# Three buffers instead of two for the keys, queries and values of a head pair

## The chip, the cores and the metric

The kernel runs on one core of a Trainium2 chip (trn2). Such a core has TensorE (PE in the profile, PEld for its weight loads), VectorE (DVE), ScalarE (ACT), GpSimd (POOL), SyncE (SP), which here only issues DMAs, and 16 DMA engines. The time is the device time of one execution in microseconds (us). The profile is a record of one such execution.

## What is computed

Three layers on 1536 tokens (2 batches of 768), in float32: attention with 8 heads of 64, in which a query sees itself and the `n_local` - 1 = 95 positions before it, and the first `n_global` = 8 keys; an MLP with a normalised input; and a layer of 8 experts, of which each token takes one.

```python
rel = pos[:, None] - pos[None, :]
is_global = pos[None, :] < int(n_global)
is_local = (rel >= 0) & (rel < int(n_local))
...
scores = scale * np.matmul(q, k.transpose(0, 1, 3, 2)) + bias   # bias: -slope of the head * distance
scores = np.where(is_global | is_local, scores, -1000000000.0)
a = np.exp(scores - np.max(scores, axis=-1, keepdims=True))
a = a / (np.sum(a, axis=-1, keepdims=True) + 1e-09)
x = np.matmul(a, v)                       # then heads side by side: 1536 x 512
...
xn = x / rms * rms_g
x = (silu(xn @ w_gate) * (xn @ w_val)) @ w_out          # 512 -> 1536 -> 512
...
out[mask] = gate_w[mask, None] * (np.maximum(x[mask] @ w1[e], 0.0) @ w2[e])   # expert e's tokens
```

## The kernel before

**Tiling.** The tokens are cut into 12 tiles of 128 rows and the tiles into six stages of two (`SIZES`). The attention works on a stage and a pair of heads at a time: 6 stages x 4 head pairs = 24 pairs, numbered 0 to 23 in the order `order`. A unit is one tile of a pair, so there are 48. A tile of queries needs at most two blocks of 128 keys: its own, and the one before it, of which the first 32 columns are replaced by the global keys.

**One pair.** `prep(gi)` makes pair gi ready. Its loads put transposed keys into `kn`, transposed queries into `qn`, and values into `vn`, in which two further columns are set to one by POOL (L432), so that the value matmuls also give the sums of the exponentials. Pairs 0 to 7 are "raw": scores come straight from `kn` and `qn` in float32 (L533, L537, L538). For pairs 8 to 23 each operand is split into a rounded part, copied by ACT (L486 keys, L498 queries), and a remainder (POOL L489 for the keys, DVE L499 for the queries), in `kt` and `qt`; the scores are then L550. POOL copies the windows with the global keys and values (L421).

**Buffers.** Pairs 0 to 3 are loaded at the very start into row tiles of the later output (`part`) that are still unused. From pair 4 on `kn`, `qn` and `vn` come from tags with two buffers each. `prep(0)` asks for the loads of pairs 4 and 5, and `prep(gi)` from gi = 4 on for those of pair gi + 2. A load can be issued when the last reader of the tile that had the buffer is through: for `kn` of a raw pair its score matmuls, of a later pair its copy and remainder; for `vn` the pair's value matmuls.

**One unit.** `scores` (TensorE, into the two banks "s"), a fused add and minimum on DVE (L557), the exponential on ACT (L561); two units later `turn`, four or two transposes on TensorE (L572) and a copy by ACT (`ptS`, L580); some three units later `values` (L601) into the one bank `xp`. Behind a pair's second unit DVE adds 1e-9 to the sums, takes reciprocals (L608, L609) and multiplies (L611, one instruction for each of the two tiles) into the row tiles `part`, which are the halves of `duo`. When four pairs of a stage are done, `tail` normalises the rows, transposes them (L400) and splits them (L403, L404) for the MLP.

**Order.** All DMAs of the attention and of the weights are issued from SP's one queue. Each engine takes its instructions in a fixed order. This order is laid down when the program is built: a planner (`schedule_with_timeline_sim=True`, L1375) goes through the program text in its order, simulates the engines, and puts an instruction into its engine's queue when its inputs and its buffer are free in that simulation. Between the units of the attention the text has steps of the first MLP pass (`moe_block`, L769 and L806) for stages whose rows are ready; steps that convert the MLP's weights (`convert64`, L334 to L354, raw data in the ring of tiles "raw", three buffers) are put in at fixed units. For the first 16 units TensorE also runs filler matmuls (`warm`).

**At the start**, before the branch that begins the body, DVE and POOL make the distance tables from two scalars that a DMA brings; `tri_f`, a triangle of ones, is made by POOL and cast to `tri` by DVE (L137, L138, L142), for the routing much later. The global keys are loaded in float32 into `kgn` in `prep(0)` and are split in `prep(2)` (L451, L452).

Of the kernel before, what the change touches and what calls it, by code (L numbers as in the profile page):

```python
# [8 lines left out]
F32 = mybir.dt.float32  # L9
# [5 lines left out]
ALU = mybir.AluOpType  # L15
# [4 lines left out]
P = 128  # L20
B, H, S, D = 2, 8, 768, 64
NT, DM, DFF = B * S, H * D, 1536
NE, DF2 = 8, 1024
KD = DM // P
NP = H // 2
# [4 lines left out]
STARTS = [sum(SIZES[:i]) for i in range(len(SIZES))]  # L30
NSTAGE = len(SIZES)
ST = ST_MAX = max(SIZES)
STAGE = ST * P
TB = S // P
VW = 2 * (D + 1)
NM = DFF // P
GW = 32
# [8 lines left out]
def kernel(  # L46
# [16 lines left out]
    nc = tc.nc  # L63
    slope = [2.0 ** (-(h + 1)) for h in range(H)]
    NFP, LATE = 4, 8
    NRAWG = 8
    XT = "ccccss"
    RING = "ccceewweec"
# [8 lines left out]
    NRAW = 3  # L77
# [24 lines left out]
    const = ctx.enter_context(tc.tile_pool(name="const", bufs=1))  # L102
# [16 lines left out]
        out=nval, in0=nneg, scalar=4294967296.0, in1=nf[:, :, 0], op0=ALU.mult, op1=ALU.add  # L119
# [7 lines left out]
        out=flagf[:, 2:3], in0=nval[0:1, 1:2], scalar=float(LMAX), in1=flagf[:, 1:2], op0=ALU.is_le, op1=ALU.mult  # L127
# [5 lines left out]

    gB = const.tile([P, DM], F32, name="gB")
    rg = const.tile([P, KD, NE], F32, name="rg")
    tri_f = const.tile([P, P], F32, name="tri_f")
    nc.gpsimd.memset(tri_f, 1.0)  # L137
    nc.gpsimd.affine_select(  # L138
        out=tri_f, in_=tri_f, pattern=[[1, P]], compare_op=ALU.is_gt, fill=0.0, base=0, channel_multiplier=-1
    )  # L140
    tri = const.tile([P, P], BF16, name="tri")
    nc.vector.tensor_copy(tri, tri_f)  # L142
    ones = const.tile([P, P], BF16, name="ones")
    nc.vector.memset(ones, 1.0)
    ie_i = const.tile([P, NE], I32, name="ie_i")
# [21 lines left out]
    rp = ctx.enter_context(tc.tile_pool(name="rp", bufs=1))  # L167

    def behind(i, first):

        tc.add_manual_dep(
            i.ins, first.ins.name,
            mybir.DependencyInfo(mybir.DependencyClass.NoSync, mybir.DependencyReason.DATA), reason="order",
        )


    def warm(n, after=None):
        for _ in range(n):
            w = psum.tile([P, 512], F32, tag="mm", bufs=NMM, name="warm")
            i = nc.tensor.matmul(  # L180
                out=w.rearrange("p (a n) -> p a n", a=4), lhsT=wz, rhs=wz.unsqueeze(1).to_broadcast([P, 4, P]),
                start=True, stop=True,
            )
            if after is not None:
                behind(i, after)
# [13 lines left out]
    def is_raw(st, hp):  # L199
        return st * NP + hp < NRAWG  # L200

    def load_pair(st, hp, kn, qn, vn):
        b, t0, nt = STARTS[st] // TB, STARTS[st] % TB, SIZES[st]
        i0 = 0 if t0 else 1
        nk = nt + 1 - i0
        k0 = (t0 - 1 + i0) * P
        hd = slice(P * hp, P * (hp + 1))
        if is_raw(st, hp):
            nc.sync.dma_start(out=kn[:, 0:nk * P], in_=kT[b][hd, k0:k0 + nk * P])
            nc.sync.dma_start(out=qn[:, 0:nt * P], in_=qT[b][hd, t0 * P:(t0 + nt) * P])  # L210
            nc.sync.dma_start(
                out=rows_of(vn)[:, i0:i0 + nk, 1:P + 1],
                in_=v[b, k0:k0 + nk * P, hd].rearrange("(t p) c -> p t c", p=P),
            )
            return kn, qn, vn
        for x, src in ((kn[:, 0:2 * nk * P], kT[b][hd, k0:k0 + nk * P]), (qn[:, 0:2 * nt * P], qT[b][hd, t0 * P:(t0 + nt) * P])):
            for r in range(2):
                nc.sync.dma_start(
                    out=x[D * r:D * (r + 1), :].rearrange("d (j s) -> d j s", j=2),
                    in_=src.rearrange("(j d) s -> d j s", j=2),  # L220
                )
        nc.sync.dma_start(
            out=rows_of(vn)[:, i0:i0 + nk, 1:P + 1],
            in_=v[b, k0:k0 + nk * P, hd].rearrange("(t p) c -> p t c", p=P),
        )
        return kn, qn, vn
# [7 lines left out]
    duo = [rp.tile([P, 2, DM], F32, name=f"duo{i}") for i in range(TT // 2)]  # L234
    part = [duo[i // 2][:, i % 2] for i in range(TT)]
# [46 lines left out]
    for x in (tab0, tabL, tabG):  # L282
        half = const.tile([P, x.shape[1]], F32, name="half" + str(len(tabs)))
        nc.scalar.activation(out=half, in_=x, func=ACTF.Copy, scale=0.5)
        tabs.append((x, half))

    warm(WARM0)
    fast = nc.values_load(flag, min_val=0, max_val=1)

    def body(is_fast):  # L290
# [9 lines left out]
        def ps(tag, bufs, name):  # L300
            return psum.tile([P, 512], F32, tag=tag, bufs=bufs, name=name)
# [108 lines left out]
        def fast_attention(pool):  # L410
            kg = pool.tile([P, NP, 2, GW], F32R, name="kg")

            kgr = pool.tile([P, NP, GW], F32, name="kgr") if NRAWG > NP else None
            kgn = pool.tile([P, NP, 2, GW], F32, name="kgn")
            vg = pool.tile([P, P], F32, name="vg")
            groups = []
            loaded = list(first_pairs)
# [5 lines left out]
            def prep(gi):  # L423
                st, hp = order[gi]
                t0, nt = STARTS[st] % TB, SIZES[st]
                i0 = 0 if t0 else 1
                n = nt * P
# [6 lines left out]
                for gn in nxt:  # L434
                    if gn >= len(order):
                        break
                    nat = [
                        pool.tile([P, 2 * STAGE if x == "q" else 2 * DM if x == "k" else (ST_MAX + 1) * VW], F32, tag=f"{x}n", bufs=2, name=f"{x}n") for x in "kqv"
                    ]
                    loaded.append(load_pair(*order[gn], *nat))  # L440
                nk = nt + 1 - i0
                if gi == 0:
                    kg0 = kT[0].rearrange("(h d) s -> d h s", d=D)[:, :, 0:GW]
                    for r in range(2):
                        nc.sync.dma_start(
                            out=kgn[D * r:D * (r + 1)].rearrange("d a j s -> d (a j) s"), in_=kg0
# [3 lines left out]
                if gi == 2:  # L450
                    nc.scalar.activation(out=kg, in_=kgn, func=ACTF.Copy)  # L451
                    nc.gpsimd.tensor_tensor(  # L452
                        out=kg[D:P], in0=kgn[D:P], in1=kg[D:P].bitcast(F32), op=ALU.subtract
# [4 lines left out]
                f = 1 if t0 >= 2 else 3 - t0  # L458
# [34 lines left out]
                if hi_dve[1]:  # L493
                    nc.vector.tensor_scalar(
                        out=qhi, in0=srq, scalar1=0.125 / slope[2 * hp], scalar2=None, op0=ALU.mult
                    )
                else:
                    nc.scalar.activation(out=qhi, in_=srq, func=ACTF.Copy, scale=0.125 / slope[2 * hp])  # L498
                lo_eng[kq[1]].scalar_tensor_tensor(  # L499
                    out=qt[:, :, 1, 0:n], in0=srq, scalar=0.125 / slope[2 * hp], in1=qhi.bitcast(F32),  # L500
# [84 lines left out]
            def values(g, t, ptf, nb):  # L585
                st, t0, hp, qt, kt, vn, vx, mx = groups[g]
                nt = SIZES[st]
                if t == 0:
                    xps[g] = ps("x", 1, "xp")
                xp = xps[g]  # L590
                for j in range(2):
                    c = slice(j * (D + 1), (j + 1) * (D + 1))
                    o = xp[:, t * VW + j * (D + 1):t * VW + (j + 1) * (D + 1)]
                    for a in range(nb):
                        if nb == 1 or a == 1:
                            rhs = vn[:, t + 1, c]
                        elif t0 + t == 1:
                            rhs = vn[:, t, c]
                        else:
                            rhs = vx[:, t, c]  # L600
                        nc.tensor.matmul(  # L601
                            out=o, lhsT=ptf[:, (j * nb + a) * P:(j * nb + a + 1) * P], rhs=rhs,
                            start=(a == 0), stop=(a == nb - 1),
                        )
                if t == nt - 1:
                    rc = pool.tile([P, ST, 2], F32, tag="rc", bufs=2, name="rc")
                    xs3 = xp[:, 0:nt * VW].rearrange("p (t c) -> p t c", c=VW)
                    nc.vector.tensor_scalar(out=rc[:, 0:nt], in0=xs3[:, :, 0:VW:VW - 1], scalar1=1e-9, scalar2=None, op0=ALU.add)  # L608
                    nc.vector.reciprocal(rc[:, 0:nt], rc[:, 0:nt])  # L609
                    for tt in range(nt):  # L610
                        nc.vector.tensor_tensor(  # L611
                            out=part[STARTS[st] + tt][:, hp * P:(hp + 1) * P].rearrange("p (j d) -> p j d", j=2),
                            in0=xp[:, tt * VW + 1:tt * VW + 1 + P].rearrange("p (j d) -> p j d", j=2),
                            in1=rc[:, tt].unsqueeze(2).to_broadcast([P, 2, D]), op=ALU.mult,
                        )
                    groups[g] = None

            warm(WARM1)
            prep(0)
            yield "work"  # L620
            tails = []
            q1, q2 = [], []
            n = hold = 0
            while n < len(units) or q1 or q2:
# [18 lines left out]
                if last is not None:  # L643
                    g, t = last
                    if t == SIZES[g // NP] - 1 and g % NP == NP - 1:
                        st = g // NP
# [518 lines left out]
        while True:  # L1165
# [12 lines left out]
            while True:  # L1178
                if moe is None and ready:
                    st = ready.pop(0)  # L1180
# [45 lines left out]
        for a in range(KD):  # L1226
            raw = rp.tile([P, P, NE], F32, tag="raw", bufs=NRAW, name="rawg")
            nc.sync.dma_start(out=raw, in_=r_gate[a * P:(a + 1) * P, :].partition_broadcast(P))
            for h in range(2):
                nc.scalar.activation(  # L1230
                    out=rgb[h][:, :, a * P:(a + 1) * P],
                    in_=raw[:, :, 4 * h:4 * h + 4].rearrange("p d e -> p e d"), func=ACTF.Copy,
# [33 lines left out]
        st, ms = NSTAGE - 1, range(M1, NM)  # L1266
        prep_next(0, first, len(first))
        banks["mm"] = MMC.split()
        with tc.manual_schedule(engines={mybir.EngineType.PE}):
# [10 lines left out]
            x = expert_tile(w1t[0], w2t[0], tka, wta, xsa, lambda: None, True)  # L1280
# [21 lines left out]
        for e in range(NE):  # L1302
# [17 lines left out]
            if e == 0:  # L1320
                x = expert_tile(w1t.pop(0), w2t.pop(0), tks[:, 0:1], wts[:, 0:1], xs.pop(0), between)
# [58 lines left out]
```

## Time and profile before

| | |
|---|---|
| Median of 3 runs | 655.97 us (655.12 to 656.81) |
| Profiled execution | 655.69 us |
| Its span in the trace | 654.0 us, so 1.69 us lie around it |
| TensorE busy | 628.9 us, 96% of the span |
| DVE, ACT, POOL busy | 446.2, 320.3, 208.7 us |
| Mean granted clock of TensorE | 0.988 of full speed |

The times of the trace are counted from the start of the span. A row of the timeline gives the start, the length (to the end of the last, where several alike are merged), the engine, the line, the operation with what it writes and reads, and in brackets how long the engine stood idle before it and what ended that. Ends of matmuls are modelled, so a busy TensorE is not one at its peak.

### The profile page before, as it was taken

To read this page: it belongs to the slowest core of one execution; us is meant where nothing else is said; L and a number is where in the kernel's file an instruction comes from. 1 tells how busy PE (TensorE), PEld (TensorE's weight loads), DVE (VectorE), ACT (ScalarE), POOL (GpSimd) and SP (SyncE) were. 2 spreads that over 40 slices of the span, in tenths; PEclk is the share of its full clock that TensorE was granted. 3 is DMA by queue.
4 is the path that set the end of the run, shared out by engine and by line. 5 is a ranking of instruction groups with operands and counts; after the bars stand their busy time and mean duration, and the time that the engine had idled before them with its cause. 6 is when DMAs were issued, how large, how long until landed. Compare 5 with 4: busy or idle time off the path is not lost. (4 is left out here: it accounts for less than half of the span.)

```text
span 654.0 us, 11691 instructions
## 1 busy us (share of the span) xinstructions
PE 628.9 (96%) x4280; PEld 562.3 (86%) x4281; DVE 446.2 (68%) x1098; ACT 320.3 (49%) x624; POOL 208.7 (32%) x275
## 2 busy tenths in 40 slices
PE   9998998899999999999999999999999999999992
PEld 4667887899999999999999999997888899899891
DVE  5765888976599988676359998944667464664410
ACT  3666798777555533334622221333656564654420
POOL 4415758663122212111222532461610221011010
PEclk9999899899999999999999999999999999999997
DMA  7536466551044532131311010442978667454000
GB/s 228 158 90 201 127 174 181 157 149 39 1 130 130 161 98 72 59 98 65 129 65 65 2 65 34 122 138 82 301 261 261 206 217 253 168 189 140 17 13 30
DMA packets 56567, 82.98 MB, mean 127 GB/s; under 512 B 7983, under 2 KB 38703, under 8 KB 56496
## 3 DMA queue, kind: packets, MB, share of 16 engines
q1 hardware_dynamic: 53552, 74.75, 36.9%
q0 software_dynamic: 2944, 7.35, 3.4%
q8 instruction: 37, 0.61, 0.4%
q14 instruction: 34, 0.28, 0.1%
HBM read 75.75 MB, written 7.39 MB: 127 GB/s over the span
## 5 line engine op out<-in xcount | busy, mean ns | idle before, releaser
L769 PE MATMUL pg<-xn,gv 128*128 128x256 f32 x1728 | 228.2, 285 | 1.2 <-DVE th L778 1.2
L769 PEld LDWEIGHTS pg<-xn,gv 128*128 128x128 f32 x1728 | 220.2, 192 | 8.2 <-DVE th L778 1.5
L787 POOL TENSOR_TENSOR hid<-hf,hid 128x256 fp32r<-128x256 f32 x72 | 61.4, 855 | 174.6 <-ACT hid L786 174.5
L806 PE MATMUL po<-ow,hid 128*128 128x512 f32 x432 | 113.9, 394 | 0.0
L1017 PE MATMUL py<-ew,eh 128*128 128x512 f32 x384 | 91.2, 395 | 0.9 <-DVE eh L1084 0.5
L1017 PEld LDWEIGHTS py<-ew,eh 128*128 128x128 f32 x384 | 71.3, 188 | 17.7 <-DVE eh L1084 0.9
L806 PEld LDWEIGHTS po<-ow,hid 128*128 128x128 f32 x432 | 75.5, 189 | 11.7 <-POOL hid L787 0.3
L1039 PE MATMUL ph<-xs,ew 128*128 128x256 f32 x672 | 83.1, 283 | 0.0
L1039 PEld LDWEIGHTS ph<-xs,ew 128*128 128x128 f32 x672 | 81.6, 191 | 0.7
L786 ACT ACTIVATE hid<-hf 128x256 fp32r<-128x256 f32 x72 | 29.9, 417 | 83.7 <-DVE hf L782 81.9
L1024 POOL DMA_INDIRECT out_dram<-yo,tk x16 | 16.5, 1034 | 139.1 <-ACT yo L1023 107.7
L838 DVE CUSTOM_DVE_ANT_0 jk<-duo,rgb 128x512 bf16<-128x512 f32 x64 | 54.3, 849 | 0.5
L561 ACT ACTIVATE pr<-pr,mx 128x256 f32<-128x256 f32 (+1 forms) x96 | 45.1, 484 | 14.0 <-DVE mx L557 13.2
L957 DVE TENSOR_TENSOR ew<-rawe,ew 128x1024 fp32r<-128x1024 f32 (+1 forms) x36 | 40.8, 1134 | 12.9 <-ACT ew L953 12.9
L1048 DVE SCALAR_TENSOR_TENSOR eh<-ph,eh 128x256 fp32r<-128x256 f32 x56 | 23.1, 423 | 37.5 <-ACT eh L1047 35.5
L777 ACT ACTIVATE th<-pg 128x256 f32<-128x256 f32 x72 | 27.2, 379 | 39.8 <-PE pg L769 37.3
L957 DVE TENSOR_TENSOR ew<-duo,ew 128x1024 fp32r<-128x1024 f32 x28 | 34.1, 1224 | 17.9 <-ACT ew L953 16.8
L953 ACT ACTIVATE ew<-rawe 128x1024 fp32r<-128x1024 f32 x36 | 38.0, 1059 | 10.2 <-PE pg L769 4.6
L778 DVE SCALAR_TENSOR_TENSOR th<-th,pg 128x256 f32<-128x256 f32 x72 | 29.7, 415 | 16.4 <-ACT th L777 15.4
L1047 ACT ACTIVATE eh<-ph 128x256 fp32r<-128x256 f32 x56 | 21.2, 384 | 39.2 <-PE ph L1039 38.1
L953 ACT ACTIVATE ew<-duo 128x1024 fp32r<-128x1024 f32 x28 | 29.4, 1059 | 19.4 <-PE py L1017 19.4
L815 DVE TENSOR_TENSOR duo<-duo,po 128x512 f32<-128x512 f32 x36 | 23.4, 684 | 18.7 <-PE po L806 18.6
(178 smaller groups left out, 935.8 us busy)
## 6 DMA issues: line engine op xcount, KB each, us to landing
rawe<-in_moe_w_dram SPq DMA_DIRECT2D x36, 512.0 KB, 5.0
duo<-in_moe_w_dram SPq DMA_DIRECT2D x28, 512.0 KB, 5.4
raw<-in_moe_w_gate_dram SPq DMA_DIRECT2D x12, 512.0 KB, 3.8
raw<-in_moe_w_val_dram SPq DMA_DIRECT2D x12, 512.0 KB, 5.6
raw<-in_moe_w_out_dram SPq DMA_DIRECT2D x12, 512.0 KB, 3.4
kn<-in_k_dram SPq DMA_DIRECT2D x28, 192.0 KB, 3.3
qn<-in_q_dram SPq DMA_DIRECT2D x36, 128.0 KB, 2.9
vn<-in_v_dram SPq DMA_DIRECT2D x16, 192.0 KB, 2.6
```

The source lines that it names most:

```text
L561: pin["act"] = nc.scalar.activation(out=pr[:, j, 0:n], in_=pr[:, j, 0:n], func=ACTF.Exp, bias=mx[:, t, j:j + 1], scale=-1.0,)
L769: nc.tensor.matmul(out=pg[:, 0:n_], lhsT=gv[:, i, a, kk, :], rhs=x[st][:, kk, :], start=(n == 0), stop=(n == 3 * KD - 1),)
L777: pin["th"] = nc.scalar.activation(out=th, in_=pss[0][:, 0:n_], func=ACTF.Tanh, scale=0.5)
L778: nc.vector.scalar_tensor_tensor(out=th, in0=th, scalar=1.0, in1=pss[0][:, 0:n_], op0=ALU.add, op1=ALU.mult)
L786: nc.scalar.activation(out=hh[:, 0], in_=hf, func=ACTF.Copy)
L787: nc.gpsimd.tensor_tensor(out=hh[:, 1], in0=hf, in1=hh[:, 0].bitcast(F32), op=ALU.subtract)
L806: nc.tensor.matmul(out=po, lhsT=hid[mi][:, a, t * P:(t + 1) * P], rhs=ow[:, c, :], start=(mi == 0 and n == 0), stop=(mi == len(ms) - 1 and ...
L838: nc.vector.tensor_tensor_reduce(out=jk, in0=part[i0 + t], in1=rgb[e // 4][:, e % 4, :], scale=1.0, scalar=0.0, op0=ALU.mult, op1=ALU.add, ...
L953: cp = nc.scalar.activation(out=t[:, 0], in_=raw, func=ACTF.Copy)
L957: nc.vector.tensor_tensor(out=t[:, 1, 0:nd], in0=raw[:, 0:nd], in1=t[:, 0, 0:nd].bitcast(F32), op=ALU.subtract)
L1017: last_mm["py"] = nc.tensor.matmul(out=py, lhsT=hid(m, a, j), rhs=w2t[m // 2][:, c, (m % 2) * DM:(m % 2 + 1) * DM], start=(n == 0), stop=( ...
L1039: nc.tensor.matmul(out=ph[:, 0:CAP], lhsT=w1t[kk][:, a, m * P:(m + 1) * P], rhs=x[:, kk, :], start=(n == 0), stop=(n == 3 * KD - 1),)
```

## The change

- The tags of `kn`, `qn` and `vn` have three buffers each (`NKN`, `NQN`, `NVN`). `kn` is cut from 1024 to 768 columns, which is what three key blocks of two heads need. What `prep` asks for, and when, stays: pair gi + 2.
- `kgn` is no tile of its own; it lies in the first 256 columns of row tile 2.
- `tri_f` is made after the tables, in a tile of the ring "raw", which is used there for the fourth time (after `ri`, `rel` and `keep`).
- A pair's two products L611 become one instruction over both tiles, 128 x 256 elements.

```diff
+    NKN, NQN, NVN = 3, 3, 3
...
-    tri_f = const.tile([P, P], F32, name="tri_f")
-    nc.gpsimd.memset(tri_f, 1.0)
-    nc.gpsimd.affine_select(
-        out=tri_f, in_=tri_f, pattern=[[1, P]], compare_op=ALU.is_gt, fill=0.0, base=0, channel_multiplier=-1
-    )
...
-    nc.vector.tensor_copy(tri, tri_f)
...
+    tri_f = rp.tile([P, P], F32, tag="raw", bufs=NRAW, name="tri_f")
+    nc.gpsimd.memset(tri_f, 1.0)
+    nc.gpsimd.affine_select(
+        out=tri_f, in_=tri_f, pattern=[[1, P]], compare_op=ALU.is_gt, fill=0.0, base=0, channel_multiplier=-1
+    )
+    nc.vector.tensor_copy(tri, tri_f)
...
-            kgn = pool.tile([P, NP, 2, GW], F32, name="kgn")
+            kgn = part[2][:, 0:2 * NP * GW].rearrange("p (a j s) -> p a j s", a=NP, j=2)
...
                     nat = [
-                        pool.tile([P, 2 * STAGE if x == "q" else 2 * DM if x == "k" else (ST_MAX + 1) * VW], F32, tag=f"{x}n", bufs=2, name=f"{x}n") for x in "kqv"
+                        pool.tile([P, w], F32, tag=f"{x}n", bufs=nb, name=f"{x}n")
+                        for x, w, nb in (
+                            ("k", 2 * (ST_MAX + 1) * P, NKN), ("q", 2 * STAGE, NQN), ("v", (ST_MAX + 1) * VW, NVN)
+                        )
                     ]
...
-                    for tt in range(nt):
-                        nc.vector.tensor_tensor(
-                            out=part[STARTS[st] + tt][:, hp * P:(hp + 1) * P].rearrange("p (j d) -> p j d", j=2),
-                            in0=xp[:, tt * VW + 1:tt * VW + 1 + P].rearrange("p (j d) -> p j d", j=2),
-                            in1=rc[:, tt].unsqueeze(2).to_broadcast([P, 2, D]), op=ALU.mult,
-                        )
+                    nc.vector.tensor_tensor(
+                        out=duo[st][:, :, hp * P:(hp + 1) * P].rearrange("p t (j d) -> p t j d", j=2),
+                        in0=xs3[:, :, 1:P + 1].rearrange("p t (j d) -> p t j d", j=2),
+                        in1=rc[:, 0:nt].unsqueeze(3).to_broadcast([P, nt, 2, D]), op=ALU.mult,
+                    )
```

## Rows read from the trace of the kernel before

**Rows 1.** Stretches of the span: busy us (instructions) of PE, PEld, DVE, ACT, POOL; clock, DMA.

```profile
60.00:110.00 50.00, 45.03 (x342) 41.69 (x342) 40.93 (x130) 40.40 (x91) 33.24 (x48) 0.97 0.61 166
...
110.00:165.00 55.00, 51.40 (x405) 49.54 (x404) 41.27 (x126) 40.89 (x86) 32.87 (x50) 0.97 0.42 116
...
165.00:620.00 455.00, 453.39 (x3086) 415.79 (x3085) 321.10 (x682) 201.12 (x367) 114.11 (x115) 1.00 0.39 127
```

**Rows 2.** The same view in slices of 5 us.

```profile
60.00:65.00 5.00, 2.81 (x25) 2.68 (x25) 1.17 (x7) 2.72 (x6) 1.78 (x1) 1.00 0.80 221
...
65.00:70.00 5.00, 5.00 (x32) 5.00 (x32) 4.05 (x7) 4.65 (x11) 4.04 (x8) 0.66 0.61 147
...
115.00:120.00 5.00, 2.80 (x23) 2.39 (x22) 5.00 (x10) 3.62 (x7) 3.54 (x7) 1.00 0.65 174
...
120.00:125.00 5.00, 5.00 (x29) 4.87 (x29) 5.00 (x15) 2.29 (x5) 4.24 (x5) 0.66 0.66 189
```

**Rows 3.** What PE waited for, 60 to 165 us: total, times, longest, us.

```profile
PE sp L550 <- DVE mx L557: 4.6, 7, 1.4
...
PE pp L572 <- ACT ptS L580: 2.2, 1, 2.2
...
PE pg L769 <- DVE th L778: 1.2, 1, 1.2
```

**Rows 4.** Timeline around PE's longest wait: start, length, engine, instruction, [idle before].

```profile
49.03 0.62 PE L538 MATMUL sp<-kn,qn 64*128 64x224 f32 x2
...
49.68 1.28 SPq L218 DMA_DIRECT2D kn<-in_k_dram  x2
...
56.31 0.64 PE L538 MATMUL sp<-kn,qn 64*128 64x224 f32 x4
...
57.86 2.97 SPq L218 DMA_DIRECT2D kn<-in_k_dram  x4
...
62.24 0.84 ACT L486 ACTIVATE kt<-kn 128x768 fp32r<-128x768 f32 x1 [2.43 <-DMA kn<-in_k_dram]
...
64.02 0.44 PE L572 MATMUL pp<-ident,pr 128*128 128x128 f32 x2 [2.19 <-ACT ptS L580]
...
64.27 0.58 ACT L403 ACTIVATE xn<-trx 128x512 fp32r<-128x512 f32 x1
```

**Rows 5.** What POOL and ACT waited for, 25 to 175 us.

```profile
POOL vn L432 <- DMA vn<-in_v_dram: 19.0, 13, 4.6
...
ACT kt L486 <- DMA kn<-in_k_dram: 3.3, 2, 2.4
```

**Rows 6.** What PE's weight loads waited for, 25 to 175 us.

```profile
PEld sp L550 <- POOL kt L421: 1.1, 1, 1.1
...
PEld sp L550 <- POOL vx L421: 1.0, 1, 1.0
```

**Rows 7.** DVE's timeline around one pair's two products (L611).

```profile
89.70 0.49 DVE L611 TENSOR_TENSOR duo<-xp,rc 128x128 f32<-128x128 f32 x2
...
90.10 0.42 DVE L557 CUSTOM_DVE_ANT_0 pr<-sp,half 128x256 f32<-128x256 f32 x1
...
90.44 0.09 DVE L557 DVE_READ_ACCUMULATOR2_ANT mx<- 128x1 f32 x1
```

**Rows 8.** DVE's timeline at the start, tri's cast and the end of the tables.

```profile
2.05 0.46 DVE L142 CAST tri<-tri_f 128x128 bf16<-128x128 f32 x1 [0.48 <-POOL tri_f L138]
...
9.44 0.17 DVE L825 CAST meta<-tok 128x12 uint32<-128x12 int32 x1 [0.54 <-DVE tab L278]
```

**Rows 9.** L499 by line and tile (ns: least, middle, most), and one meeting with L489.

```profile
L499 DVE SCALAR_TENSOR_TENSOR qt<-qn,qt 128x512 fp32r<-128x512 f32 x16 | 20.3, 1275 | 4.2 <-ACT qt L498 4.2
...
L499 DVE SCALAR_TENSOR_TENSOR qt<-qn,qt x16: 680/1051/2272, 55.9 to 148.2; 128x512 fp32r<-128x512 f32 x16
...
67.16 1.83 POOL L489 TENSOR_TENSOR kt<-kn,kt 64x768 fp32r<-64x768 f32 x1
...
67.26 2.27 DVE L499 SCALAR_TENSOR_TENSOR qt<-qn,qt 128x512 fp32r<-128x512 f32 x1 [0.89 <-ACT qt L498]
```

## The prediction

> **What bounds the kernel now.** I read the table of long stretches first, then short slices of the stretch that stood out, then who TensorE waited for there, then the timeline around its longest wait. From 165 to 620 us TensorE is busy for 453.39 of 455 us at full clock [rows 1]: nothing that this change touches lies there. The weak stretch is 60 to 165 us, where the attention of pairs 8 to 23 is mixed with the first layer of the MLP: 105 us less 96.43 busy is 8.57 us of idle TensorE [rows 1]. In two slices of 5 us the granted clock is 0.66 [rows 2], and both stand right behind a slice in which TensorE was busy for only 2.8 us. [...] So 8.57 + 2 x 1.70 = 12.0 us are to be had in this stretch, and hardly more anywhere else.
>
> Who ended those waits [rows 3]: DVE, late in emptying a score bank (4.6 us) and late with a gate (1.2), and ACT with one copy (2.2, once). The last is the longest single wait, and the timeline shows what it is [rows 4]. At 59.81 ACT's next instruction is the copy of pair 9's keys (L486). It stands waiting 2.43 us for their DMA and starts at 62.24. Behind it in ACT's order are an exponential and the copy ptS that TensorE's next transposes need; TensorE goes on at 64.02, after 2.19 us. The DMA was issued at 57.86. What held it is read from the score matmuls on kn (L538), eight instructions to each of the pairs 4 to 7: the last of pair 6 are the two at 49.03, over at 49.65, and the last of pair 7 are among the four at 56.31, over at 56.95. Pair 8's keys were issued at 49.68, 0.03 us after pair 6 was done; pair 9's came after pair 7. With two buffers each pair waits for the one two before it.
>
> **The change part by part.**
>
> *Third buffer, keys and queries.* Pair 9 then takes the place of pair 6 (tiles 4, 5, 6 are the first three), free at 49.65, not at 56.95. Its load may be issued some 8 us earlier. From issue to the waiting copy took 62.24 - 57.86 = 4.38 us, so it is there at about 54.1, against 59.81 when ACT wants it: 5.7 us to spare. The wait of 2.43 us on ACT goes, and with it TensorE's 2.19, and the low clock of the next slice, 1.70: **3.89 us**. What is late next is TensorE's own queue: the row copy L403, which the next MLP block needs, stood on ACT behind the same wait and came at 64.27. Later pairs gain little: the only other wait of ACT for keys is 3.3 - 2.43 = 0.9 us [rows 5], and TensorE is not seen waiting for it, so I take it at nothing; if it were all TensorE's it would be 0.9.
>
> *Third buffer, values.* POOL waits 19.0 us in 13 places for vn's DMA before it writes the ones columns (L432) [rows 5], because a load can't be issued before the last value matmuls of the pair two before it. Value matmuls run about two and a half pairs behind the scores (two queues, LAG1 2 and LAG2 3), so one pair more, some 6 us at 16 pairs in 105 us, covers the longest POOL wait of 4.6. Behind that memset on POOL stand the window copies of values and keys and, for the next pair, the subtraction L489; ACT, TensorE and the tail's pow wait for those. But TensorE's own waits [rows 3] name neither POOL nor these; only its weight loads do, 1.1 + 1.0 us [rows 6]. I take nothing for it: the freed time is POOL's, which is busy 66.1 of 105 us. Bounds: nothing, to 2.1 us gained.
>
> *SP's queue.* No DMA is added; 16 pairs issue the same five loads of about 0.6 us each. Loads that no longer wait let those of the weights, which stand behind them in the one queue, pass earlier. Nothing, either way.
>
> *One product for two.* 24 instructions of 256 elements replace 48 of 128. Two of the old ones take 0.49 us together, and the next instruction begins 0.40 after the first [rows 7]. The new shape (four dimensions, PSUM source, broadcast factor) isn't in the trace; nearest is DVE's 256-wide read of PSUM right behind it, 0.42 us to its end and 0.34 from start to start [rows 7]. Saved per pair: between 0.40 - 0.34 = 0.06 and, should nothing of the second old one have been hidden, 0.49 - 0.34 = 0.15 us. For the 16 pairs of the stretch, 1.0 to 2.4 us of DVE, which is busy for 82.2 of the 105 us. It is worth something only where TensorE waits for DVE (5.8 us there); a lower end of 7% of it (5.8 / 82.2), an upper end of all. I take 0.5 us. The one bank xp is also freed 0.06 to 0.15 sooner; no TensorE wait names it, so nothing more. [...]
>
> *kgn in row tile 2, tri_f in the "raw" ring.* kgn is read in pair 2's preparation, and row tile 2 is first written by pair 4's product, behind four more units of scores: nobody waits. tri_f's two POOL instructions and DVE's cast (0.46 us) move from the start, where both engines wait for the two scalars, to behind the tables. There DVE stands idle for 0.54 us after its last table [rows 8], which hides the cast. Nothing; uncovered, 0.46 us lost. POOL's two are needed by that cast alone. The ring's fourth tile takes the place of ri, which is read out before the tables are made; the weights' raw loads come after it in SP's order: nothing.
>
> *The order itself.* The planner lays out every engine's queue anew, with its own idea of when loads land. That can't be priced from a row; it is the reason for the width.
>
> **Sum.** The profiled execution took 655.69 us (span 654.0 and 1.69 around it). 655.69 - 2.19 - 1.70 - 0.5 = 651.3 us. The median of the runs shown, 655.97, is 0.28 above it: a gain of 0.7% against either. Differences within 0.3% (2.0 us, 654.0 to 658.0) are what a measurement of this kernel can't tell from no change.
>
> **Rivals.**
> *The wait moves to DVE (no change).* With loads no longer last, the queues of DVE and ACT are. Both are 80% busy from 60 to 110 us [rows 1], and in the second weak place DVE is busy for all of 115 to 120 [rows 2], and none of TensorE's waits but the one of 2.2 us leads to a load. If TensorE's waits for DVE grow from 5.8 to 9.7 us, the 3.89 are back: 655.2. For it: that place. Against it: DVE is busy for only 1.17 us of the slice with the stall [rows 2], and TensorE has MLP work to put there.
>
> *POOL against DVE (slower).* The query remainder on DVE (L499) takes 680 ns at best and 2272 at worst, 1275 on average [rows 9]. The worst began 0.10 us after POOL's subtraction L489 (1.83 us) and ended 0.54 us after it [rows 9]: it was held until POOL was through. POOL without its waits may start L489 beside L499 more often. If all 16 were held as long as the worst, DVE would have 16 x 1.0 = 16 us more; at 0.6 us of TensorE waiting per us so lost (5.8 waited now, for 16 x 0.595 = 9.5 lost), that is 9.6, and with 4.4 gained the time is 660.9. It turns slower than no change above a mean of about 1275 + 4400 / 0.6 / 16 = 1730 ns. Against it: L499 follows ACT's two copies as L489 follows the first, before and after. [...]
>
> *Everything opens (larger gain).* Pairs prepared a whole pair earlier let scores run ahead, DVE's late places vanish too: 655.69 - 12.0 = 643.7. Against it: DVE's work stays.
>
> **How the numbers follow.** Forecast case, 648 to 653.9: 0.48. Larger gain, 643.7 to 648: 0.14. No change: 0.22. Slower, 658 to 661: 0.16. Faster is 0.48 + 0.14 = 0.62. The range takes the forecast, the no-change case to its edge of 658, and the nearer half of the larger gain, to 645.5; left out are 0.07 below and about 0.13 above. The forecast's own range is 648 to 653.9.
>
> **What the profile after would show.** Right: pair 9's L218 issued near 50 us; no ACT wait for kn over 1 us; TensorE idle in 60 to 165 us near 6 us, not 8.6, and full clock from 65 to 70; POOL's waits on vn's DMA under 5 us; 24 products of about 0.4 us. Wrong: these gone, and TensorE's waits for DVE above 8 us (moved), or L499 above 1.7 us on average (held by POOL), or a third slice at a low clock. The prediction would also fail if the planner drew the score matmuls forward so that loads are last again.

## The result, and the profile after

The changed kernel took 661.22 us (median of 8 runs, 658.23 to 671.06), the kernel before 655.72 beside it (8 runs): a ratio of 1.0065, 95% interval 1.0038 to 1.0092. It is slower, by 4.3 us, and outside the range of the prediction. The profiled execution, the shortest of the eight, took 658.23 us, with a span of 656.5 us and a mean granted clock of 0.980 (before 654.0 and 0.988). Medians of time are over all runs; ratios, the medians of span and clock further down, and the medians that the expectations name leave out runs more than 1.5% above the fastest of their kernel (654.3 us for all_in_old_order, where the table has 655.71).

The stretches of [rows 1] in the changed kernel, with the same columns:

```profile
60.00:110.00 50.00, 47.37 (x367) 43.58 (x367) 41.95 (x130) 40.07 (x91) 29.98 (x45) 0.96 0.58 159
110.00:165.00 55.00, 52.87 (x403) 50.84 (x402) 41.49 (x119) 40.75 (x87) 32.75 (x50) 0.94 0.38 100
165.00:620.00 455.00, 451.90 (x3075) 413.99 (x3074) 318.30 (x680) 200.56 (x365) 117.51 (x115) 1.00 0.39 126
```

TensorE's idle time from 60 to 165 us fell from 8.57 to 105 - 47.37 - 52.87 = 4.76 us, more than the prediction asked for; but 1.46 us of idle have come up just ahead of that stretch. The third column from the end, the granted clock, got worse. In slices of 5 us, as in [rows 2]:

```profile
50.00:55.00 5.00, 3.54 (x27) 3.08 (x25) 3.87 (x10) 2.13 (x4) 3.05 (x4) 0.85 0.78 184
55.00:60.00 5.00, 5.00 (x26) 3.94 (x22) 1.77 (x6) 3.35 (x6) 3.28 (x5) 0.50 0.73 220
60.00:65.00 5.00, 5.00 (x29) 3.98 (x30) 1.67 (x8) 1.50 (x3) 0.65 (x2) 0.62 0.57 165
65.00:70.00 5.00, 5.00 (x46) 5.00 (x45) 4.44 (x15) 4.81 (x11) 2.40 (x4) 1.00 0.42 119
115.00:120.00 5.00, 2.99 (x17) 2.53 (x17) 5.00 (x12) 4.91 (x12) 4.67 (x8) 0.84 0.38 104
120.00:125.00 5.00, 5.00 (x25) 5.00 (x25) 5.00 (x11) 2.15 (x5) 2.70 (x4) 0.50 0.48 124
```

The slice behind the old stall, 65 to 70, is at full clock now. But 55 to 60 and 120 to 125 are wholly at half of full speed (0.50), and 50:55, 60:65 and 115:120 partly: 0.75 + 2.5 + 1.9 + 0.8 + 2.5 = 8.45 us lost, an estimate from this column, where [rows 2] gave 3.4. As before there are two low stretches, one behind a single wait early on and one behind idle time just ahead of 120 us; each is longer now. In steps of 1 us the clock was below 1.00 from 65 to 69 and from 120 to 124; in the changed kernel it is so from 53 to 64 and from 118 to 126. What stands ahead of the first long stretch is in the timeline:

```profile
47.32 0.17 DVE L614 RECIPROCAL rc<-rc 128x4 f32<-128x4 f32 x1
...
48.32 1.49 DVE L504 SCALAR_TENSOR_TENSOR qt<-qn,qt 128x512 fp32r<-128x512 f32 x1 [0.82 <-ACT qt L503]
...
49.28 2.60 SPq L213 DMA_DIRECT2D kn<-in_k_dram  x4
...
49.73 1.75 DVE L345 SCALAR_TENSOR_TENSOR cv<-raw,cv 128x512 uint32<-128x512 uint32 x1
...
51.41 0.41 DVE L615 TENSOR_TENSOR duo<-xp,rc 128x256 f32<-128x256 f32 x1
...
51.87 0.44 PE L606 MATMUL xp<-vx,ptS 128*128 128x65 f32 x2 [1.46 <-DVE duo L615]
```

The reciprocal of a pair was over at 47.49, and its product could have followed. In DVE's new queue pair 8's query remainder (L504) and a step of the weights (L345) stand between it and the product, which therefore came at 51.41. TensorE stood 1.46 us for the bank xp, and its clock fell behind that (the slices from 50 to 65).

The marks that the prediction set, by groups of waits (25 to 175 us) and by line:

```profile
POOL vn L434 <- DMA vn<-in_v_dram: 8.4, 10, 2.2
ACT kt L491 <- DMA kn<-in_k_dram: 3.1, 2, 1.6
```

```profile
L504 DVE SCALAR_TENSOR_TENSOR qt<-qn,qt 128x512 fp32r<-128x512 f32 x16 | 21.3, 1330 | 4.2 <-ACT qt L503 4.2
L615 DVE TENSOR_TENSOR duo<-xp,rc 128x256 f32<-128x256 f32 x24 | 10.1, 420 | 0.4
```

POOL's waits for values fell from 19.0 to 8.4 us [rows 5]. The copy L491 still waits up to 1.6 us for keys, but no longer with TensorE behind it. L504 takes 1330 ns on average, near the 1275 of before, and a merged product 420 ns. The waits for loads that the sum priced are gone from TensorE, and the kernel is slower.

Every run reports its span and mean granted clock. Span times clock is an estimate of the span had every microsecond been at full clock (1.00); the rest is what the clock took. It counts low clock while TensorE idles as lost too: the idle end of the span, at 0.5 in the profiles, makes 4 to 6 us of it. Medians over the runs: before 647.5 and 7.9 us (128 runs beside the experiments), after 644.0 and 15.8. **By this estimate the change saved 3.5 us of work and waits, near the 2.7 that the sum had for them (2.19 + 0.5), and the clock took 8 us more.** The two profiled executions alone give 654.0 x 0.988 = 646.2 and 656.5 x 0.980 = 643.4: 2.8 us saved, and 5.3 us more for the clock.

### The profile page after: what moved, and what is told of

The parts are those of the page before. It is cut to its first block, busy times and chain, and to the rows that moved or that the text cites. A ratio compares the mean times of both kernels' runs of the same rounds, so it can differ in the third digit from the quotient of the medians.

```text
span 656.5 us, 11654 instructions
## 1 busy us (share of the span) xinstructions
PE 632.0 (96%) x4280; PEld 564.6 (86%) x4281; DVE 444.0 (68%) x1074; ACT 319.4 (49%) x624; POOL 213.0 (32%) x275
## 5 line engine op out<-in xcount | busy, mean ns | idle before, releaser
L791 POOL TENSOR_TENSOR hid<-hf,hid 128x256 fp32r<-128x256 f32 x72 | 63.0, 877 | 177.1 <-ACT hid L790 176.8
L957 ACT ACTIVATE ew<-rawe 128x1024 fp32r<-128x1024 f32 x36 | 38.0, 1057 | 10.6 <-PE pg L773 4.6
```

Source lines behind the costliest of these rows:

```text
L791: nc.gpsimd.tensor_tensor(out=hh[:, 1], in0=hf, in1=hh[:, 0].bitcast(F32), op=ALU.subtract)
L957: cp = nc.scalar.activation(out=t[:, 0], in_=raw, func=ACTF.Copy)
```

## The experiments

All but the first row were timed over five rounds beside the kernel before (656.6 to 657.4 us). "Own" order is what the planner made of that kernel. A ratio below 1 is faster than before, and is told from no change where its interval leaves out 1.

| Kernel | Buffers k,q / v | Products | Order of the queues | Median us | Ratio to before, 95% | Span x clock | Lost to clock |
|---|---|---|---|---|---|---|---|
| after | 3 / 3 | one | own | 661.22 | 1.0065 [1.0038, 1.0092] | 644.0 | 15.8 |
| prod_only | 2 / 2 | one | own | 661.51 | 1.0085 [1.0057, 1.0112] | 647.9 | 11.9 |
| no_merge | 3 / 3 | two | own | 655.60 | 0.9973 [0.9952, 0.9994] | 645.7 | 7.5 |
| kq_two | 2 / 3 | one | own | 661.18 | 1.0071 [1.0047, 1.0094] | 647.6 | 11.9 |
| queue_behind | 3 / 3 | one | own, L504 later | 654.32 | 0.9963 [0.9940, 0.9986] | 644.7 | 7.8 |
| swap_two | 2 / 2 | two, swapped | own | 660.70 | 1.0062 [1.0041, 1.0084] | 649.3 | 10.6 |
| swap_three | 3 / 3 | two, swapped | own | 656.26 | 0.9996 [0.9971, 1.0022] | 646.5 | 7.9 |
| behind_two_products | 3 / 3 | two | own, L504 later | 653.82 | 0.9950 [0.9931, 0.9970] | 645.2 | 6.2 |
| behind_two_buffers | 2 / 2 | one | own, L504 later | 665.70 | 1.0113 [1.0073, 1.0154] | 648.0 | 15.3 |
| all_in_old_order | 3 / 3 | one | of before | 655.71 | 0.9968 [0.9939, 0.9997] | 646.8 | 7.8 |
| buffers_in_old_order | 3 / 3 | two | of before | 654.33 | 0.9948 [0.9927, 0.9968] | 646.6 | 6.2 |
| product_in_old_order | 2 / 2 | one | of before | 657.19 | 1.0001 [0.9974, 1.0027] | 647.6 | 7.9 |
| two_products_new_order | 3 / 3 | two | of after | 660.15 | 1.0043 [1.0016, 1.0070] | 646.2 | 12.2 |
| all_in_order_of_two | 3 / 3 | one | of no_merge | 655.77 | 0.9996 [0.9976, 1.0016] | 645.9 | 7.2 |
| one_product_earlier | 3 / 3 | one | of after, but one | 658.90 | 1.0025 [1.0005, 1.0045] | 644.6 | 11.5 |
| one_product_later | 3 / 3 | one | of before, but one | 661.83 | 1.0080 [1.0060, 1.0101] | 646.3 | 13.2 |
| products_at_once_new | 3 / 3 | one | of after, but 12 | 663.05 | 1.0061 [1.0034, 1.0087] | 647.0 | 11.5 |
| products_at_once_old | 3 / 3 | one | of before, but 13 | 654.80 | 0.9972 [0.9945, 0.9999] | 646.3 | 6.5 |

**One part at a time, each in its own order.** My first theory was the clock behind the one wait at 51 us (clock theory); the rivals were that the merged product is to blame (product theory), and that POOL holds up L504 on DVE (lock theory).

prod_only: the kernel before, with one edit.

```diff
-                    for tt in range(nt):
-                        nc.vector.tensor_tensor(
-                            out=part[STARTS[st] + tt]...
+                    nc.vector.tensor_tensor(
+                        out=duo[st][:, :, hp * P:(hp + 1) * P]...
```

> The kernel before with one product for two and nothing else of the change. Clock theory (pair 8 prepared earlier puts its query remainder in front of pair 4's product on DVE; TensorE waits, and its clock then stays low for some 10 us): two buffers, so pair 8 is as late as before; 653.5 to 656.5 us, mean granted clock 0.986 or more, one low stretch of 3 to 4 us after the wait at 62. Product theory (the merged product itself is what delays TensorE): 658 or more. Lock theory (DVE's query remainder held more often by POOL): as before, 655.5 to 656.5.

no_merge: the changed kernel with the diff above undone.

> The changed kernel with two products for each pair again: three buffers and the moves of kgn and tri_f. Clock theory: pair 8 is prepared early as in the changed kernel, a wait for the bank xp near 50 us and a low clock for some 10 us behind it; 658 to 663 us, mean clock 0.982 or less. Product theory: 651 to 655. Lock theory: 657 to 661, with a mean of the query remainder above 1300 ns.

kq_two:

```diff
-    NKN, NQN, NVN = 3, 3, 3
+    NKN, NQN, NVN = 2, 2, 3
```

> The changed kernel with two buffers for keys and queries and three for values only. Clock theory: pair 9's keys are late as before (ACT waits some 2.4 us for them near 60 us), no low stretch at 53; 653.5 to 656.5 us, mean clock 0.986 or more. Lock theory (POOL, freed of its waits on the values' loads, meets DVE more): 657 to 661. Product theory: 657 or more.

queue_behind: the changed kernel, with L504 queued behind the last product traced before it.

```diff
-                lo_eng[kq[1]].scalar_tensor_tensor(
+                lo = lo_eng[kq[1]].scalar_tensor_tensor(
...
+                behind(lo, last_product[0])
```

> The changed kernel with each pair's query remainder queued on DVE behind the product traced last before it (an order of issue only). Clock theory: no TensorE wait of over 1 us near 50 us, no low clock from 53 to 64; 651 to 654.5 us, mean clock 0.985 or more. Lock theory: POOL's and DVE's meetings go on, 657 or more. Product theory: 657 or more.

The clock theory met queue_behind alone, and the lock theory none of the four. The product theory met prod_only and kq_two, and missed no_merge (655.60) by 0.6 us. But queue_behind has merged products and is fast, so the product alone can't be it. And the order of TensorE's matmuls changed with the product: the planner had laid out every queue anew. Both kernels with two key buffers kept a long wait for a load: prod_only that of [rows 4], 2.64 us to 64.06, with ACT's copy of keys 2.94 us late; kq_two one of 2.35 us to 61.85, behind ACT's copy of the queries:

```profile
60.77 0.63 ACT L503 ACTIVATE qt<-qn 128x512 fp32r<-128x512 f32 x1 [2.13 <-DMA qn<-in_q_dram]
```

The two with three have no wait of over 1 us there.

**A new order with no new work.** swap_two is the kernel before with a pair's two products emitted in reversed order; swap_three is no_merge with the same. No work is added or taken away.

```diff
-                    for tt in range(nt):
+                    for tt in reversed(range(nt)):
```

> Kernel before, with the two normalising products of a pair in reversed order; no work is added or removed, but the planner's order changes on TensorE, VectorE and ScalarE. Order theory (a re-planned order alone moves the time by several us, through which waits arise and how long the clock stays low): at least 2 us away from before, on either side, 650 to 665 us; the wait for the keys at 62 to 64 us stays, since keys have two buffers. Product theory (only a merged product is late): within 1.5 us of before, 655 to 658 us.

> Three buffers and the moves, two products, these in reversed order; no work added or removed against the kernel with three buffers and two products (655.6 us). Order theory: at least 2 us away from it, 650 to 664 us. Product theory: within 1.5 us of it, 654 to 657 us. Both: no wait of over 1 us on TensorE at 62 to 64 us, since keys have three buffers.

swap_two is 0.62% slower, nearly as much as the whole change. This row is its stretch from 60 to 110 us:

```profile
60.00:110.00 50.00, 42.24 (x308) 38.17 (x307) 38.53 (x131) 39.16 (x88) 31.41 (x44) 0.95 0.62 163
```

TensorE is busy for 42.24 us of it, where [rows 1] had 45.03. A price for "order" of about 4 us is thus shown without any edit of substance. Not all was as the order theory expected: ACT still waits 2.28 us for keys (to 64.56), but in this order TensorE has other work, and its longest wait there is 0.87 us. swap_three can't be told from before, and is 0.66 us above no_merge: the order theory's 2 us failed there. Two more, with L504 queued as above:

> Three buffers, the moves, two products, and the query remainder put behind the last product on VectorE. Product theory: the merged product was the only cost and the edit takes it away already, so with two products the edit finds nothing to mend: 654 to 657 us, as without it (655.6). Order theory: a further re-planned order, which can fall either way by several us: 650 to 664 us.

> Kernel before with the merged product and the query remainder behind it; two buffers everywhere. Product theory, in its form that lateness of the product is what costs: the edit brings it back to before, 655 to 658 us, and the wait at 62 to 64 us stays. Product theory, in its form that the merged product itself costs: 660 to 663 us as without the edit (661.5). Buffer theory (three key buffers are worth about 2 to 4 us whatever the order): 2 to 4 us above the same kernel with three buffers (654.3), 656 to 658 us.

behind_two_buffers, at 665.70, lies above the ranges of all three theories, and behind_two_products, at 653.82, just below the product theory's; the order theory's range was too wide to be tested by it. By the ratios the queueing rule gave 1.0% in the changed kernel. With two products it gave 0.23%, and with two buffers it cost 0.28%, and neither is clear of the intervals. It is no remedy, only another draw of the order. Over these nine own orders, the medians of span times clock part the kernels: 647.6 to 649.3 us with two key buffers, 644.0 to 646.5 with three. What the clock takes follows neither the buffers nor the product: it is lowest and highest, 6.2 and 15.8 us, with three buffers.

**The same edits with the order held still.** For the next five each engine's queue, SP's DMA issues among them, was fixed to the list of another kernel, by dependencies of the class NoSync; a merged product stands where the second of its two stood. PLAN is that list. No run holds a kernel to its own list, so what the holding itself costs is not measured; product_in_old_order, at 1.0001, comes nearest to it.

```diff
+    def queue_as(plan):
+        ...
+            for a, b in zip(queue, queue[1:]):
+                tc.add_manual_dep(
+                    traced[b], a,
+                    mybir.DependencyInfo(mybir.DependencyClass.NoSync, mybir.DependencyReason.DATA), reason="order",
+                )
...
+            queue_as(PLAN)
```

> The whole change, but each engine's queue and the DMA queue keep the order of the kernel before: every instruction is queued behind the one that stood ahead of it there, and a merged product stands where the second of its two stood. This is the change as the prediction priced it, with the order unchanged. Order theory (the parts are worth what the prediction said, and the re-planned order took it back): 650 to 653.5 us, TensorE's wait at 62 to 64 us gone. Rival, that the third buffer only helps when the loads' places in the queues move too: 654.5 to 657 us, the wait at 62 to 64 us still there.

> Three buffers and the moves with two products, in the order of the kernel before on every queue. Order theory: 651 to 654 us, half a microsecond above the same with merged products. Rival (the loads' places must move too): 655 to 657 us, as before.

> The merged product alone, in the order of the kernel before on every queue. Order theory: the 4.6 us that the merged product cost by itself (661.5 against 656.9) came from the re-planned order, so 655 to 657.5 us. Product theory (a merged product is late, since it needs both tiles and holds the bank): 660 to 663 us.

> The changed kernel with two products again, but each queue in the order of the changed kernel; the two products stand where the merged one stood. Order theory: the order keeps its cost, 659.5 to 663 us, with TensorE's wait near 51 us and the low clock behind it. Product theory: without the merged product 654 to 657 us.

> The whole change with merged products, in the order that the planner gave the same kernel with two products (655.6 us). Order theory: 653.5 to 656.5 us. Product theory: 659 to 663 us.

The order theory met the last three. In the first two the time lies above its range (655.71 against 653.5 at most, 654.33 against 654), in the rival's for the first, but the wait at 62 to 64 us, which the rival for the first kept, is gone in both. The merged product, 0.85% slower in its own order, costs nothing in the old one (1.0001). The buffers give 0.52%, 3.4 us (2.1 to 4.8), in the order of before. The whole change is 0.32% faster there, 2.1 us (0.2 to 4.0), and 0.65% slower in its own: 0.97%, 6.4 us, for the order alone. With two products the changed kernel's order still costs, 1.0043 against no_merge's 0.9973. In all_in_order_of_two, too, the merged product is not slow (0.9996); the interval doesn't tell it from no_merge. The slices of all_in_old_order where [rows 2] shows the stall:

```profile
60.00:65.00 5.00, 5.00 (x47) 5.00 (x46) 3.56 (x14) 5.00 (x11) 4.08 (x6) 1.00 1.09 223
65.00:70.00 5.00, 5.00 (x46) 5.00 (x44) 4.27 (x10) 4.16 (x12) 4.67 (x8) 1.00 0.71 178
```

TensorE is busy throughout, at full clock, where it had 2.81 us and then 0.66: this is the kernel that the prediction priced, though it gains 2.1 us and not 4.4. two_products_new_order shows the other side, its slices and then its wait:

```profile
50.00:55.00 5.00, 3.19 (x15) 2.29 (x14) 4.26 (x9) 2.91 (x6) 2.81 (x4) 0.77 0.68 172
55.00:60.00 5.00, 5.00 (x23) 3.87 (x24) 1.61 (x8) 1.75 (x3) 3.40 (x4) 0.50 0.46 110
60.00:65.00 5.00, 5.00 (x25) 3.87 (x24) 2.07 (x6) 2.11 (x4) 1.09 (x3) 0.50 0.81 226
```

```profile
53.02 0.69 PE L621 MATMUL xp<-vx,ptS 128*128 128x65 f32 x2 [1.76 <-DVE duo L631]
```

The wait for a product and the long low clock come with the order, merged or not.

**One instruction.** In the next two all queues are held, and one product on DVE is moved: in the changed kernel's order ahead of L504 and L345, in the order of before behind L577, L360, L577 and L363 (these lines are 15 higher in the kernels with a fixed order). The cut shows DVE's queue, not the text of the kernel.

```diff
 (order of after)
 RECIPROCAL
+product
 L504
 L345
-product
...
 (order of before)
-product
 L577
 L360
 L577
 L363
+product
```

> The changed kernel with every queue in its own order, but for one instruction: the product that TensorE waits for at 51 us stands two places earlier on VectorE, ahead of the query remainder (1.49 us) and the weights' step (1.75 us). Theory of the one wait (the 1.46 us wait at 51.9 us starts the low clock of 53 to 64 us, which costs 5 us more): that wait and that stretch go, 653.5 to 657 us. Rival theory (the low clock comes at the next wait in any case, so that only the wait itself is saved): 659 to 661.5 us.

> The whole change in the old order (654.3 us), but for one instruction: the product of the same pair stands four places later on VectorE, behind two steps of the weights and two of the scores, so that TensorE should wait for it some 1.5 us at 50.6 us. Theory of the one wait: 658 to 662 us, with a long stretch of low clock from 52 to 54 us on. Rival: the wait itself alone, 655 to 657 us.

one_product_later is slower by 1.12% than all_in_old_order (1.0080 against 0.9968): 7.4 us for one instruction of 0.41 us. From its timeline, and its slices:

```profile
48.79 0.16 DVE L629 RECIPROCAL rc<-rc 128x4 f32<-128x4 f32 x1
...
51.58 1.20 DVE L363 SCALAR_TENSOR_TENSOR cv<-raw,cv 128x512 uint32<-128x512 uint32 x1
...
52.70 0.41 DVE L630 TENSOR_TENSOR duo<-xp,rc 128x256 f32<-128x256 f32 x1
...
53.16 0.44 PE L621 MATMUL xp<-vx,ptS 128*128 128x65 f32 x2 [1.43 <-DVE duo L630]
```

```profile
55.00:60.00 5.00, 5.00 (x18) 2.95 (x18) 2.22 (x8) 2.86 (x5) 2.96 (x5) 0.53 0.95 216
60.00:65.00 5.00, 5.00 (x37) 4.46 (x35) 1.52 (x6) 2.29 (x5) 0.72 (x2) 0.78 0.89 216
```

The wait is 1.43 us, and the slow clock behind it takes 5 x (0.47 + 0.22) = 3.5 us in this execution; the median lost to the clock rises from 7.8 to 13.2 us. So one late product can cost what the changed kernel lost. How that divides into waits and clock is less sure: between the two profiled executions the clock makes only some 1.4 us of 5.7, as all_in_old_order's has low slices of its own, elsewhere. one_product_earlier fell to 658.90 us (2.6 us less by the ratios), on the rival's edge. The wait and the low clock at 53 us are gone from its slices, but others are there, and the first of them stands ahead of the moved product, behind a wait of 1.82 us at 22.80 (0.34 in the profile of the changed kernel): the moved product can't have made it. The slices:

```profile
25.00:30.00 5.00, 5.00 (x17) 2.87 (x15) 2.71 (x9) 2.38 (x5) 1.45 (x3) 0.50 0.58 189
...
50.00:55.00 5.00, 4.48 (x23) 2.42 (x22) 3.43 (x9) 3.16 (x6) 3.38 (x5) 1.00 0.59 175
55.00:60.00 5.00, 4.94 (x42) 4.35 (x41) 4.26 (x13) 2.14 (x4) 3.63 (x4) 1.00 0.85 195
...
120.00:125.00 5.00, 4.29 (x20) 4.29 (x21) 5.00 (x10) 3.19 (x10) 4.74 (x7) 0.56 0.49 137
```

**All products at once.** Then each product was put directly behind its reciprocal, in both orders.

```diff
 RECIPROCAL
+product
...
-product
```

> The changed kernel in its own order on every queue, but each pair's product stands directly behind its reciprocal on VectorE; 12 of the 24 move up by one or two places. If the late products near 51 and 118 us (each behind a step of the weights on VectorE) are what the new order costs: 653.5 to 656.5 us, both waits and the low clock behind them gone. If only the one near 51 us counted, or other waits take over: 658 to 660 us, as with that one product alone (658.9).

> The whole change in the order of the kernel before, with each product directly behind its reciprocal; 13 of the 24 move up. If lateness of the product costs in this order too: 1 us or more below the same without it (654.3), 650 to 653.3 us. If no wait of TensorE there led to a product: no change, 653.5 to 656 us.

Neither helped: 1.0061 in the changed kernel's order, above both ranges, and 0.9972 in the old one, the case of no change. In the profiled execution of products_at_once_new (666.07 us, against the median of 663.05) TensorE reaches other late work instead:

```profile
79.55 0.76 PE L570 MATMUL sp<-kt,qt 128*128 128x256 f32 x4 [2.00 <-DVE mx L577]
...
129.77 0.80 PE L570 MATMUL sp<-kt,qt 128*128 128x256 f32 x2 [1.36 <-DVE mx L577]
```

The theory that late products in general are the cost of the new order falls. That one of them can cost this much (in the order of before) is shown, and that the order as a whole does; which of its places make up the rest in the changed kernel stays open.

## Why the prediction was wrong

*Third buffer for keys and queries, -3.89 us.* Right. In the order of before, buffers and moves together give 3.4 us (2.1 to 4.8), and the wait and the low slice at 62 to 70 us are gone. In the changed kernel pair 9's keys are issued at 49.28 us ("near 50"), TensorE's idle time is 4.76 ("near 6"), 65 to 70 us is at full clock. Only "no wait of ACT for keys over 1 us" is wrong: ACT waits 1.60 us for pair 8's and 1.46 for pair 9's, whose copy the new order wants at 53.8 us and not at 59.81.

*Values, 0.* POOL's longest wait is 2.2 us, as foretold. kq_two and prod_only, which differ by the values' buffer and the moves, are 661.18 and 661.51; each has its own order, so this doesn't isolate it.

*One product, -0.5.* Its length was right (420 ns). Alone in the old order it gives 0.0 us (-1.7 to +1.8), which neither shows nor excludes the half microsecond.

*The moves of kgn and tri_f, 0.* Not run alone; they are inside buffers_in_old_order.

*"The order itself ... can't be priced from a row; it is the reason for the width."* This is the step that failed. The order got no term of its own and was taken as spread around the sum, and the width then came from other cases: no rival had a worse order in it, and the 0.16 for slower was all POOL's lock on DVE. Held still, the buffers' part comes out, and the whole change gains 2.1 us (0.2 to 4.0), less than the 4.4 of the sum but the way it said. Laid out anew, the same parts cost 6.4 us more, and a swap of two equal instructions costs 4. The 1.70 us for the low clock, in the sum once and in the 12.0 us twice, is an estimate, 5 x (1 - 0.66) from the slice in [rows 2]; no run shows it as a gain by itself. In steps of 1 us from 65 to 69 the clock there was 0.74, 0.50, 0.50 and 0.55; TensorE had 6 or 7 matmuls in a step at 0.50, and 11 or 12 in each of the next three at 1.00. In the changed kernel that slice did recover, but by the estimate above the kernel as a whole lost 8 us more to the clock. The prediction's own mark, "a third slice at a low clock", is what the trace shows.

*The rivals.* None came true as written. L504 is at 1330 ns, far from the 1730 at which the lock would decide by the prediction's estimate. In both traces nine of the 16 query remainders run beside a subtraction on POOL (L489, L354; L494, L356 after) and end 0.54 to 0.56 us after it, with 0.99 to 2.35 us each; the other seven take 0.68 to 0.99 us. So such meetings were no more frequent than before. TensorE's waits for DVE's mx from 60 to 165 us fell from 4.6 to 0.7 us, where the rival wanted 9.7 for DVE in all (the view of [rows 3]). By the same view two longer waits now end with POOL's copying of windows (L423), which [rows 3] doesn't name and which the prediction took at nothing:

```profile
PE sp L555 <- POOL kg L423: 1.3, 1, 1.3
PE xp L606 <- POOL kt L423: 1.3, 1, 1.3
PE sp L555 <- DVE mx L562: 0.7, 3, 0.3
```

In both a DVE instruction ended within 0.2 us before POOL's, so the view doesn't show POOL alone to be late. The second, to 118.57 us, is the wait ahead of the low clock from 118 to 125.

Six versions are faster than both kernels by their intervals. The fastest two, three buffers and two products in the order of before (0.9948), and the same parts in their own order with L504 behind the last product (0.9950), can't be told apart.

## What to carry to other kernels

Where a planner lays out the queues, an edit's time is its own effect plus a new draw of the order. Here the draw cost up to 1%, or nothing that could be told; no run shows one that gained on the order of before. Before crediting or blaming an edit of that size, time an edit that changes nothing but the order, and time the edit itself with every queue held to the old list. In one_product_later the low clock behind a wait of TensorE's took more than the wait itself (3.5 us behind 1.43), so a good order deserves to be kept when buffers are added.

## What was not expected of the hardware

A wait's length didn't tell what the clock would do. In product_in_old_order TensorE has a wait of 2.65 us, longer than the 2.19 of [rows 4], and then full clock:

```profile
64.89 0.44 PE L587 MATMUL pp<-ident,pr 128*128 128x128 f32 x2 [2.65 <-ACT ptS L595]
```

```profile
60.00:65.00 5.00, 2.35 (x22) 2.15 (x20) 1.70 (x9) 2.11 (x5) 0.91 (x1) 1.00 0.82 218
65.00:70.00 5.00, 5.00 (x44) 5.00 (x45) 3.56 (x6) 5.00 (x12) 4.42 (x7) 1.00 0.71 180
```

In the changed kernel 1.46 us of waiting went ahead of a stretch at 0.50 of full speed that shows in three slices (0.85, 0.50, 0.62). The prediction's reading, that a slice with 2.8 us of work is followed by one at 0.66, holds for the two of [rows 2] and not for this one with 2.35. The same program also varies: over seven runs of the changed kernel the clock took from 11.8 to 18.6 us, while span times clock stayed within 642.4 to 645.3.
